# Splitting the first weight load and moving two small loads ahead of ScalarE's barrier

## The chip, the cores and the metric

The kernel runs on one core of a Trainium2 chip. The metric is the device time of one execution, in microseconds (us). The profile of an execution gives a span that is about 1.3 us shorter than its time (436.1 against 437.44 us for the first profiled execution). Repeated executions of one kernel agree within about 0.3%. A few lie near 445 us; they count as slow and are left out of every ratio. The medians quoted for a kernel are over all its runs; without the slow ones they would be lower by at most 0.27 us, which changes no verdict.

Short names: PE is TensorE's matmul side and PEld its weight loads, DVE is VectorE, ACT is ScalarE, POOL is GpSimd, SP is SyncE. A name with q (SPq, ACTq) is that engine's sequencer, which issues DMAs.

## The reference, cut to what matters

One decode step for 8 rows: a modulation computed from `c`, a grouped-query attention over a long cache, then a gated MLP.

```python
mod = (silu(c) @ w_mod)            # c: 8 x 1024, w_mod: 1024 x 6144, bf16: 12.6 MB
h = layernorm(x) * (1 + ca) + sa
q = h @ wq                         # 1024 x 4096: 8.4 MB
# attention: k and v caches of 8 x 4 x 8192 x 128 each: 134.2 MB together
x = x + ga * (attention(q, k_cache, v_cache) @ wo)      # wo: 8.4 MB
h = layernorm(x) * (1 + cb) + sb
x = x + gb * ((relu(h @ W_gate) * (h @ W_up)) @ W_down) # 3 x 7.3 MB
```

Every weight and cache byte is read once: 185.6 MB for 8 rows of output.

## The kernel before

All large loads go through one ring in SBUF (`arena`, 65,536 bf16 columns on 128 partitions). SyncE issues them in a fixed order: `w_mod` in two pieces of 6.29 MB, `wq` in two of 4.19 MB, then k and v by turns (16 pieces each of 4.19 MB), then `wo` and the MLP's weights. `pump` issues a load as soon as everything that lay in its part of the ring has been read.

```python
for i in range(2):
    load(("wm", i), wm_src[:, 24 * D * i:24 * D * (i + 1)], 24 * D)   # D = 1024
for i in range(2):
    load(("wq", i), wq_src[:, 2 * i * SLOT:2 * (i + 1) * SLOT], 2 * SLOT)
# ... k and v by turns, wo, gate, up, down ...
head = stream[1:]
del stream[1:]
pump()                                                    # first w_mod piece
for t, src in enumerate((c.rearrange(...), A_x.rearrange(...))):
    P.op("sp" if t == 0 else "act", lambda e, t=t, src=src: e.dma_start(cx[:, t, :], src), ...)
stream.extend(head)
P.pump = pump
pump()                                                    # second w_mod piece, first wq piece
```

The two `w_mod` pieces and the first `wq` piece fill the ring (24 + 24 + 16 thousand columns). The second `wq` piece needs the room of the first `w_mod` piece, so it waits until PE has done the first half of the modulation. The first k and v pieces wait for the second half. The modulation itself needs `c`: PE spreads c and x over the partitions with one matmul, DVE and ACT form silu(c) and its transpose and the first layer norm, and then come the modulation's 96 matmuls, 48 for each piece of `w_mod`.

`start_loads_first` moves SyncE's first DMA ahead of everything else on that engine and the next two ahead of its barrier instruction. So in the kernel before, SyncE's queue holds the first `w_mod` piece, then c, then the second piece. ScalarE issues x after the barrier.

Of the kernel before, what the change touches and what calls it, by code (L numbers as in the profile page):

```python
# [236 lines left out]
def start_loads_first(nc, n):  # L237

    block = nc.main_func.blocks[0]
    ins = list(block.instructions)  # L240
    sp = [i for i, x in enumerate(ins) if x.engine == mybir.EngineType.SP]
    at = next(i for i in sp if ins[i].opcode == "EventSemaphore")
    first = [ins[i] for i in sp if i > at][:n]
    assert all(x.opcode == "DMACopy" and not x.sync_info.on_wait for x in first), [x.opcode for x in first]
    names = {x.name for x in first}
    rest = [x for x in ins if x.name not in names]
    at = next(i for i, x in enumerate(rest) if x.engine == mybir.EngineType.SP and x.opcode == "EventSemaphore")
    rest = rest[:at] + first[1:] + rest[at:]
    at = next(i for i, x in enumerate(rest) if x.engine == mybir.EngineType.SP)
    block.instructions = rest[:at] + first[:1] + rest[at:]  # L250


def hold_weights(nc, held):
# [6 lines left out]
def bass_adaLN_cond__gqa_block_cached__glu_gated_reglu__decode_kernel(nc, A_x, A_k_cache, A_v_cache, A_wq, A_wo, B_x, B_W_gate, B_W_up, B_W_down, c, w_mod, out):  # L260
    B, _, D = A_x.shape
# [17 lines left out]
    P = Prog()  # L279
# [7 lines left out]
    with ExitStack() as es:  # L287
        E = es.enter_context

        def sb(name, shape, dtype):  # L290
            return E(nc.sbuf_tensor(name, shape, dtype))
# [15 lines left out]
        cx = sb("cx", [32, 2, 256], dt.bfloat16)  # L307
# [53 lines left out]
        def R(t, lo=0, hi=1):  # L361
            return (t, lo, hi)
# [9 lines left out]
        stream, place, cursor = [], {}, [0]  # L372

        def load(key, src, n):
            stream.append((key, src, n))

        def pump():
            while stream:
                key, src, n = stream[0]
                lo = cursor[0] if cursor[0] + n <= RING else 0  # L380
                if P.unread("arena", lo, lo + n):
                    return
                stream.pop(0)
                cursor[0] = lo + n
                place[key] = lo
                dst = arena[:, lo:lo + n]
                if len(src.shape) == 3:
                    dst = dst.rearrange("p (a n) -> p a n", a=src.shape[1])
                P.op("sp", lambda e, dst=dst, src=src: e.dma_start(dst, src), writes=[slot_r(lo, lo + n)], dma=True,
                     own=(key[0], key[1] % 2) if key[0] in "kv" else None)  # L390
                if key[0] in "kv":
                    P.held[key] = (lo, lo + n)

        wm_src = w_mod.rearrange("(p k) n -> p (k n)", k=KC)
# [2 lines left out]
        g_src = B_W_gate.rearrange("(p k) n -> p (k n)", k=KC)  # L397
        u_src = B_W_up.rearrange("(p k) n -> p (k n)", k=KC)
        d_src = B_W_down.rearrange("(p k) n -> p (k n)", k=KF)
        for i in range(2):  # L400
            load(("wm", i), wm_src[:, 24 * D * i:24 * D * (i + 1)], 24 * D)
        for i in range(2):
            load(("wq", i), wq_src[:, 2 * i * SLOT:2 * (i + 1) * SLOT], 2 * SLOT)
        for m in range(M):
# [9 lines left out]
        wd_parts = [(0, 14), (14, 21), (21, 25), (25, 27), (27, 28)]  # L414
        for i, (r0, r1) in enumerate(wd_parts):
            load(("wd", i), d_src[:, r0 * D:r1 * D], (r1 - r0) * D)
        head = stream[1:]
        del stream[1:]
        pump()
        for t, src in enumerate((c.rearrange("b (j n) -> (b j) n", j=4), A_x.rearrange("b o (j n) -> (b o j) n", j=4))):  # L420
            P.op("sp" if t == 0 else "act", lambda e, t=t, src=src: e.dma_start(cx[:, t, :], src), writes=[R("cx", t, t + 1)], dma=True)
        stream.extend(head)
        P.pump = pump
        pump()
# [120 lines left out]
        for z in range(2):  # L545
            src = ps[:, 3 + z, :].rearrange("p (u x r) -> p u r x", u=J, r=2)
# [14 lines left out]
        for u in range(4):  # L561
            src = ps[:, 5, :].rearrange("p (t j u b) -> p u b t j", t=2, j=J, u=4)[:, u]
# [152 lines left out]
        for z in range(2):  # L715
# [9 lines left out]
            else:  # L725
                P.op("act", lambda e, dst=dst, z=z: e.activation(dst, ps[:, z, :], ACT.Copy), reads=[bank(z)],
                     writes=[("kt", 512 * z, 512 * z + 512)])
# [22 lines left out]
        def row_turn(src, src_r, t):  # L750
# [6 lines left out]
             writes=[R("xg")])  # L757
# [15 lines left out]
        for h in range(2):  # L773
            P.op("act", lambda e, h=h: e.activation(grel[:, H * h:H * h + H], ps[:, h, 0:H], ACT.Relu), reads=[bank(h)],
                 writes=[("kt", 4096 + FJ * h, 4096 + FJ * h + FJ)])
# [26 lines left out]
        P.plan()  # L802
        P.emit(nc, dict(sp=nc.sync, act=nc.scalar, pool=nc.gpsimd, dve=nc.vector, pe=nc.tensor), sems)
        start_loads_first(nc, 3)
        hold_weights(nc, holding)

# [27 lines left out]
```

## Time and profile before

| | before |
|---|---|
| time, median of 3 runs | 437.1 us |
| span of the profiled execution | 436.1 us |
| bytes read | 185.63 MB |
| PE / DVE busy | 63% / 61% |
| SyncE's DMA queue, share of 16 engines | 98.8% |

These lines are from the page of the kernel before. The second line shown gives busy time, its share and the number of instructions for each engine. The GB/s line gives the DMA rate in 40 equal slices of the span (10.9 us each), and the last line gives SyncE's queue.

```profile
span 436.1 us, 3867 instructions
...
PE 275.4 (63%) x1643; PEld 119.1 (27%) x1483; DVE 265.6 (61%) x377; ACT 29.9 (7%) x62; POOL 14.5 (3%) x32
...
GB/s 407 425 418 433 431 433 433 434 433 431 433 433 433 433 433 433 433 433 433 433 433 433 433 433 433 433 433 433 436 433 433 433 433 433 450 429 422 428 429 211
...
q1 hardware_dynamic: 6848, 185.63, 98.8%
```

The rate stands at 433 GB/s in slice after slice, while neither PE nor DVE is busy two thirds of the time.

The chain of waits, followed back from the last instruction, reads quite differently (shares of the span by engine):

```profile
PE 42%; DVE 20%; issue 12%; DMA 6%; ACT 0%; SPq 0%
```

The start, from the timeline of the kernel before (start, duration, engine, line, operation, tiles; in brackets the idle time before it and what ended that):

```profile
0.00 0.38 SPq L389 DMA_DIRECT2D arena<-in_w_mod_dram  x1
...
0.63 0.34 SPq L421 DMA_DIRECT2D cx<-in_c_dram  x1
...
0.78 0.39 ACTq L421 DMA_DIRECT2D cx<-in_A_x_dram  x1
...
1.57 31.31 SPq L389 DMA_DIRECT2D arena<-in_A_wq_dram  x2
...
17.93 0.60 PE L450 MATMUL ps<-cx,rsel 32*128 32x512 bf16 x1 [17.93 <-DMA cx<-in_c_dram]
...
27.21 8.10 PE L516 MATMUL ps<-arena,hT 128*32 128x512 bf16 x96
...
32.31 0.11 PEld L516 LDWEIGHTS ps<-arena,hT 128*32 128x32 bf16 x4 [1.55 <-DMA arena<-in_w_mod_dram]
...
35.34 0.33 SPq L389 DMA_DIRECT2D arena<-in_A_k_cache_dram  x1
...
41.98 3.61 PE L539 MATMUL ps<-arena,hT 128*32 128x512 bf16 x32 [6.67 <-DMA arena<-in_A_wq_dram]
```

c is issued at 0.63 us but PE's first matmul (L450) waits for it until 17.93 us. The modulation (L516) starts at 27.21 us; its second half starts at 32.31 us. The first k load is issued at 35.34 us, and `wq`'s matmuls (L539) wait for their weights until 41.98 us. The `wq` line covers two issues, the first at 1.57 us and the second 31 us later.

From the issue lines of the DMA view (last number: us from issue to landing), and from the waits view (us in total, times, longest):

```profile
cx<-in_c_dram SPq DMA_DIRECT2D x1, 16.0 KB, 17.3
cx<-in_A_x_dram ACTq DMA_DIRECT2D x1, 16.0 KB, 9.6
```

```profile
PE ps L450 <- DMA cx<-in_c_dram: 17.9, 1, 17.9
...
DVE kt L581 <- DVEq L181: 16.7, 10, 2.7
```

The last waits line is DVE's wait for the landing of k (line 181 is the wait on a load's own semaphore): 16.7 us in all, in 10 of the 16 turns of the loop.

### The profile page before, as it was taken

How to read it: one execution, taken by the hardware profiler on the slowest of the kernel's cores; microseconds unless marked ns; L12 is line 12 of the kernel's file. 1: busy time of each engine (PE TensorE's matmuls, PEld its weight loads, DVE VectorE, ACT ScalarE, POOL GpSimd, SP SyncE). 2: the span in 40 equal slices, each digit the busy share in tenths (PEclk: the TensorE clock that was granted, in tenths of full speed). 3: DMA queues.
4: the chain of work that ended last, by engine and by line, in shares of the span. 5: the costliest groups of instructions: out<-in, count | busy, mean ns of one | idle time of the engine just before them, and what ended most of it. 6: DMA issues, size and time to landing. Idle time of an engine off the chain costs nothing.

```text
span 436.1 us, 3867 instructions
## 1 busy us (share of the span) xinstructions
PE 275.4 (63%) x1643; PEld 119.1 (27%) x1483; DVE 265.6 (61%) x377; ACT 29.9 (7%) x62; POOL 14.5 (3%) x32
## 2 busy tenths in 40 slices
PE   0063337759595957768595968768595958546437
PEld 0010002324242333324242333323242333242005
DVE  0233048687777867677787777678878676443020
ACT  1100010010101010010101010010101010110000
POOL 7000000000000000000000000000000000000000
PEclk9998569697978969696987969698887979867658
DMA  9999999999999999999999999999999999999995
GB/s 407 425 418 433 431 433 433 434 433 431 433 433 433 433 433 433 433 433 433 433 433 433 433 433 433 433 433 433 436 433 433 433 433 433 450 429 422 428 429 211
DMA packets 6934, 185.74 MB, mean 426 GB/s; under 512 B 816, under 2 KB 912, under 8 KB 1168
## 3 DMA queue, kind: packets, MB, share of 16 engines
q1 hardware_dynamic: 6848, 185.63, 98.8%
q8 instruction: 5, 0.08, 0.1%
q10 hardware_dynamic: 80, 0.02, 0.0%
q14 instruction: 1, 0.01, 0.0%
HBM read 185.63 MB, written 0.02 MB: 426 GB/s over the span
## 4 chain that ended last, share of the span: by engine, by line
PE 42%; DVE 20%; issue 12%; DMA 6%; ACT 0%; SPq 0%
PE ps L641 20%; PE ps L592 15%; DVE kt L581 9%; DMA arena<-in_B_W_down_dram 6%; DVE negm L604 5%; PE ps L610 2%; PE ps L658 1%; PE ps L769 1%; DVE om L652 1%; PE ps L738 1%; DVE mj L615 1%; DVE mjt L618 1%; DVE negm L608 1%; DVE kt L728 0%; DVE lx L701 0%
## 5 line engine op out<-in xcount | busy, mean ns | idle before, releaser
L581 DVE STREAM_TRANSPOSE kt<-arena 128x1024 uint32<-128x1024 uint32 x128 | 149.5, 1216 | 40.3 <-PE ps L592 23.3
L641 PE MATMUL ps<-arena,pT 128*64 128x512 bf16 x512 | 94.9, 551 | 52.1 <-issue 52.1
L592 PE MATMUL ps<-kt,qpad 128*128 128x512 bf16 x512 | 120.8, 382 | 10.0 <-DVE kt L581 8.6
L641 PEld LDWEIGHTS ps<-arena,pT 128*64 128x64 bf16 x512 | 45.3, 156 | 95.6 <-issue 90.9
L592 PEld LDWEIGHTS ps<-kt,qpad 128*128 128x128 bf16 x512 | 45.5, 97 | 83.9 <-DVE kt L581 29.1
L631 DVE STREAM_TRANSPOSE pT<-prb 64x1024 bf16<-64x1024 bf16 x32 | 39.7, 1239 | 18.1 <-ACT prb L624 17.6
L624 ACT ACTIVATE prb<-ps,bias 128x1024 bf16<-128x1024 f32 x16 | 17.8, 1113 | 293.0 <-DVE mjt L618 293.0
L604 DVE TENSOR_REDUCE negm<-ps 128x1 f32<-128x512 f32 x32 | 22.1, 690 | 11.6 <-PE ps L592 11.6
L652 DVE SCALAR_TENSOR_TENSOR om<-ps,im,om 128x128 f32<-128x128 f32 x51 | 17.7, 347 | 0.7
L769 PE MATMUL ps<-arena,hT 128*32 128x448 bf16 x128 | 11.7, 546 | 9.6 <-DMA arena<-in_B_W_up_dram 5.8
L610 PE MATMUL ps<-identf,negm 128*128 128x128 f32 x32 | 7.8, 326 | 15.6 <-DVE negm L608 15.6
L658 PE MATMUL ps<-jmp,om 128*128 128x16 f32 x34 | 6.7, 273 | 17.0 <-DVE om L652 17.0
L573 POOL TENSOR_TENSOR qpad<-qR,mq 128x128 bf16<-128x128 bf16 x16 | 6.3, 398 | 318.2 <-DVE pT L631 266.9
L539 PE MATMUL ps<-arena,hT 128*32 128x512 bf16 x64 | 7.2, 631 | 14.3 <-DMA arena<-in_A_wq_dram 14.3
L776 DVE TENSOR_TENSOR kt<-ps,kt 128x448 bf16<-128x448 f32 x2 | 1.2, 620 | 20.1 <-PE ps L769 20.1
L788 PE MATMUL ps<-arena,hmT 128*32 128x256 bf16 x112 | 8.8, 323 | 5.5 <-DMA arena<-in_B_W_down_dram 5.5
L452 DVE CAST cxr<-ps 128x512 bf16<-128x512 f32 x1 | 0.7, 691 | 18.6 <-PE ps L450 18.6
L450 PE MATMUL ps<-cx,rsel 32*128 32x512 bf16 x1 | 0.6, 604 | 17.9 <-DMA cx<-in_c_dram 17.9
L550 DVE CAST kt<-ps 128x512 bf16<-128x512 f32 x1 | 0.7, 692 | 17.9 <-PE ps L539 17.9
L610 PEld LDWEIGHTS ps<-identf,negm 128*128 128x128 f32 x32 | 4.7, 187 | 23.6 <-DVE negm L608 23.6
L658 PEld LDWEIGHTS ps<-jmp,om 128*128 128x128 f32 x34 | 5.1, 188 | 20.5 <-DVE om L652 20.5
L788 PEld LDWEIGHTS ps<-arena,hmT 128*32 128x32 bf16 x112 | 6.1, 114 | 9.0 <-DMA arena<-in_B_W_down_dram 7.4
(89 smaller groups left out, 96.3 us busy)
## 6 DMA issues: line engine op xcount, KB each, us to landing
arena<-in_A_k_cache_dram SPq DMA_DIRECT2D x16, 4096.0 KB, 21.5
arena<-in_A_v_cache_dram SPq DMA_DIRECT2D x16, 4096.0 KB, 19.6
arena<-in_w_mod_dram SPq DMA_DIRECT2D x2, 6144.0 KB, 24.5
arena<-in_A_wq_dram SPq DMA_DIRECT2D x2, 4096.0 KB, 30.5
arena<-in_A_wo_dram SPq DMA_DIRECT2D x2, 4096.0 KB, 18.1
arena<-in_B_W_gate_dram SPq DMA_DIRECT2D x2, 3584.0 KB, 16.5
arena<-in_B_W_up_dram SPq DMA_DIRECT2D x2, 3584.0 KB, 20.9
arena<-in_B_W_down_dram SPq DMA_DIRECT2D x1, 3584.0 KB, 21.8
```

The lines of the kernel that those rows point to most:

```text
L539: fns.append(lambda e, w=w, z=z, g=g, kk=kk: hold(e.matmul(ps[32 * g:32 * g + 32, 3 + z, :], hT[:, kk, :], w[:, g, z, :], start=(kk == 0), ...
L581: P.op("dve", lambda e: e.transpose(ktb[:, to:to + QE].bitcast(dt.uint32), arena[:, lo:lo + QE].bitcast(dt.uint32)), reads=[slot_r(lo, lo ...
L592: fns.append(lambda e, t=t, r=r: e.matmul(ps[:, b, :].rearrange("p (c k) -> p c k", k=32), qpad[:, m % 2, t * 2 + r, 24 - 8 * i:152 - 8 * ...
L604: P.op("dve", lambda e: e.tensor_reduce(negm[:, h:h + 1], ps[:, b, :], AX.X, ALU.max, negate=True), reads=[bank(b)] + (free(("v", m - 1)) ...
L610: P.op("pe", lambda e: e.matmul(ps[:, 4, 0:128], negm[:, 2:3].to_broadcast([128, 128]), identf[:], start=True, stop=True), reads=[R("negm" ...
L624: P.op("act", lambda e: e.activation(prb[:], ps[:, 2 * z:2 * z + 2, :].rearrange("p h n -> p (h n)"), ACT.Exp, bias=bias[:, z:z + 1], scal ...
L631: P.op("dve", lambda e, g=g: e.transpose(pT[64 * g:64 * g + 64, z, :, g, :], prb[64 * g:64 * g + 64, :]), reads=[R("prb")] + ([R("qpad", z ...
L641: fns.append(lambda e, t=t: e.matmul(ps[64 * (t % 2):64 * (t % 2) + 64, 5, :].rearrange("p (i d) -> p i d", d=Dh), pT[:, z, t].rearrange(" ...
L652: P.op("dve", lambda e, i=i: e.scalar_tensor_tensor(out=om[:], in0=ps[:, 5, Dh * i:Dh * i + Dh], scalar=im[:, i:i + 1], in1=om[:], op0=ALU ...
L658: P.op("pe", lambda e: e.matmul(ps[:, 6 + z, 0:16], om[:], jmp[:].rearrange("p g j -> p (g j)"), start=True, stop=True), reads=[R("om"), R ...
L769: fns.append(lambda e, w=w, r=kk - r0, kk=kk, h=h, j=j, b0=b0: hold(e.matmul(ps[32 * j:32 * j + 32, b0 + h, 0:H], hT[:, kk, :], w[:, r, j, ...
L788: fns.append(lambda e, w=w, r=k - r0, k=k, i2=i2, j=j: e.matmul(ps[32 * j:32 * j + 32, 4, 0:256], hmT[:, k, 1 - i2:33 - i2], w[:, r, i2, j ...
```

## The change

The intent is to let c and x land at once instead of behind 6 MB, so that the modulation can start earlier. The first piece of `w_mod` becomes two DMAs: 2 KB a row (256 KB in all) ahead of the remaining 46 KB a row. While the engines work on the short rows, c and x are to slip in from ScalarE's queue, on which they are now the very first instructions.

```diff
-    rest = rest[:at] + first[:1] ...            # SyncE only: 1 DMA ahead of all, n-1 ahead of the barrier
+    for engine, ahead, total in ((SP, 1, n), (Activation, 2, 2)):
+        ...                                     # the same for ScalarE: 2 DMAs ahead of all
...
-        for i in range(2):
-            load(("wm", i), wm_src[:, 24 * D * i:24 * D * (i + 1)], 24 * D)
+        load(("wm", 0), wm_src[:, 0:D], D)
+        load(("wm0", 0), wm_src[:, D:24 * D], 23 * D)
+        load(("wm", 1), wm_src[:, 24 * D:48 * D], 24 * D)
...
-        head = stream[1:]
-        del stream[1:]
+        head = stream[2:]
+        del stream[2:]
...
-            P.op("sp" if t == 0 else "act", lambda e, t=t, src=src: e.dma_start(cx[:, t, :], src), ...)
+            P.op("act", lambda e, t=t, src=src: e.dma_start(cx[:, t, :], src), ...)
```

(The hunks are shortened; the first says what the rewritten loop does.)

## The prediction

> **What bounds the kernel now.** The stream of loads. The page's DMA lines give 185.74 MB, 98.8% of 16 engines' span for SyncE's queue, and 433 GB/s in nearly every slice; PE is busy 63%, DVE 61%. The fabric ceiling of 435 GB/s (Trainium skill, "DMA: Bandwidth & Descriptors", Specifications) agrees with the 433 measured. 185.63 MB at 433 GB/s are 428.7 of the 436.1 us. The rest is at the ends: in the packet records the first weight packet starts 1.0 us after the first issue and takes 2.4 us where later ones of its size take 1.815 us; the last weight piece lands at 432.6 us and 3.5 us of work follow (chain of waits). In between no slice shows the queue empty: each load is issued some 20 us before it lands.
>
> **What the change does.** Today c is second in SyncE's queue, behind 6 MB, and lands at 17.9 us; x goes on ScalarE's queue after the barrier (issued at 0.78, landed about 10.1 us, since its 512 B packets alternate with 48 KB packets of 1.8 us). PE waits 17.9 us for c (waits view). Afterwards both are issued between 0.0 and 0.8 us on ScalarE's queue, while the other queue holds only the 256 KB piece, eight packets of 2 KB per engine (84 ns each in the last weight piece), because the rest is issued at about 0.63 us. Engines take queues in turn, packet by packet (same page, Queues, rings and completion order; the trace agrees), so c and x should land at 2.5 to 4 us, or up to 7 us if one or two 46 KB packets slip between.
>
> Costs: one more issue (0.38 us on SyncE); the small packets, an estimate of under 0.1 us (8 x 84 ns against 8 x 76 ns by bytes); the barrier is delayed by about 0.4 us by the two issues, which moves GpSimd's setup (rsel at 1.9 us, then 2.3) and the first wq issue. A gap of up to 0.3 us is possible if the small piece drains before the rest's descriptors are there.
>
> **How much is on the critical path.** Nearly nothing. PE's first matmul (cx by rsel) moves from 17.9 to about 3 us, and the transposed input of the modulation is ready near 8 us. The first half of the modulation matmuls then waits for its 6 MB; it starts near 17 instead of 27.2 us and ends near 21.5 instead of 32 us, and the second wq load is issued 10 us earlier. But the second half already waits 1.55 us for its weights, which land at 32.3 us because of 12.6 MB at 433 GB/s. So from 32 us on everything stands as before: modulation done at 35.3 us, first k load issued then, wq matmuls at 42 us on DMA. The earlier wq issue finds a queue not empty.
>
> **Prediction:** 437.0 us, 8 in 10 between 436.0 and 438.2. Faster by over 2%: 0.01; within 2%: 0.98; slower by over 2%: 0.01.
>
> **What would show each step.** Right: PE's cx matmul before 8 us; first modulation matmul at 16 to 19 us, waiting for weights instead of DVE; second half still at 32 to 33 us on a w_mod DMA; wq matmuls at about 42 us; 433 GB/s from the second slice on; last weight landing at 432 to 433 us. Wrong: cx still late; second half not on DMA; slice 0's rate changed by over 3%.
>
> **What would make it wrong.** A gap in the old stream that the slices hide and the earlier wq issue closes (gain up to 1 us); the small piece slowing the stream's start (loss up to 1 us); the span starting earlier because ScalarE's first issue precedes SyncE's.

## The result, and the profile after

The changed kernel took 436.83 us (median of 6 runs, 436.54 to 437.17), the kernel before 437.19 us over its 6 runs. The ratio of fast runs is 0.9995, with a 95% interval from 0.9982 to 1.0009. A ratio is the mean time of one kernel's fast runs over that of the other's fast runs in the same rounds, so it is not quite the ratio of the medians quoted. The verdict is: the same.

The page of the changed kernel:

```profile
span 435.6 us, 3869 instructions
...
PE 277.4 (64%) x1643; PEld 120.8 (28%) x1483; DVE 265.8 (61%) x377; ACT 29.9 (7%) x62; POOL 14.5 (3%) x32
...
GB/s 373 438 444 433 429 433 433 434 430 432 433 433 433 433 433 433 433 433 433 433 433 433 433 433 433 433 433 433 433 433 433 433 433 433 423 429 444 428 420 233
...
q1 hardware_dynamic: 6944, 185.61, 98.9%
```

Its start (line numbers are 5 higher than before, those of loads 4):

```profile
0.00 1.44 SPq L393 DMA_DIRECT2D arena<-in_w_mod_dram  x3
0.12 0.40 ACTq L426 DMA_DIRECT2D cx<-in_c_dram  x1
...
0.56 0.44 ACTq L426 DMA_DIRECT2D cx<-in_A_x_dram  x1
...
1.58 21.29 SPq L393 DMA_DIRECT2D arena<-in_A_wq_dram  x2
...
8.57 0.58 PE L455 MATMUL ps<-cx,rsel 32*128 32x512 bf16 x1 [8.57 <-DMA cx<-in_A_x_dram]
...
17.82 4.68 PE L521 MATMUL ps<-arena,hT 128*32 128x512 bf16 x48
...
31.74 4.54 PE L521 MATMUL ps<-arena,hT 128*32 128x512 bf16 x48 [9.24 <-DMA arena<-in_w_mod_dram]
...
36.33 0.33 SPq L393 DMA_DIRECT2D arena<-in_A_k_cache_dram  x1
...
41.40 3.60 PE L544 MATMUL ps<-arena,hT 128*32 128x512 bf16 x32 [5.11 <-DMA arena<-in_A_wq_dram]
```

The issue lines and waits that answer to those of before:

```profile
cx<-in_c_dram ACTq DMA_DIRECT2D x1, 16.0 KB, 2.9
cx<-in_A_x_dram ACTq DMA_DIRECT2D x1, 16.0 KB, 7.9
```

```profile
DVE kt L586 <- PE ps L597: 26.8, 14, 3.0
...
DVE kt L586 <- DVEq L181: 12.0, 9, 2.8
...
PE ps L521 <- DMA arena<-in_w_mod_dram: 9.2, 1, 9.2
...
PE ps L455 <- DMA cx<-in_A_x_dram: 8.6, 1, 8.6
```

c now lands about 3 us after the start and x at 8.5 us. PE's first matmul moves from 17.93 to 8.57 us, 9.4 us earlier, and the modulation's first half from 27.21 to 17.82 us. Then all of the gain turns into one new wait: PE stands 9.24 us before the second half, for the second piece of `w_mod`. That half starts at 31.74 us instead of 32.31, and the first k load is issued at 36.33 us, a microsecond *later* than before.

That last point is the clock. The granted clock (PEclk) is the share of TensorE's full clock that the chip let it have. The line below is from the table of stretches, for the stretch from 32.31 to 35.35 us; before:

```profile
core 0: us, PE busy (x) PEld busy (x) DVE busy (x) ACT busy (x) POOL busy (x), PEclk, DMA share, GB/s
32.31:35.35 3.04, 3.00 (x52) 0.42 (x16) 0.00 (x1) 0.00 (x1) 0.00 (x0) 1.00 0.80 345
```

and after:

```profile
32.31:35.35 3.04, 3.04 (x36) 0.49 (x12) 0.00 (x0) 0.00 (x0) 0.00 (x0) 0.50 0.87 377
```

The columns are those of the first line; the stretch itself and its length come first. The granted clock (PEclk, third number from the end) was 1.00 before and 0.50 after. (The view counts time before a trace's first clock record as 1.00. That record starts at 32.78 us in the kernel before and only at 47.42 us in c_at_32 below.) A matmul of the modulation took 634 ns at 0.50 and 379 ns at 1.00. Before, PE ran the two halves without a pause (the first 48 matmuls took 5.1 us, the last 48 about 3.0). After the change it stood idle for 9 us between them and started the second half slowly again: 4.54 us for 48 matmuls. The Trainium skill, "TensorE: Matmul & The Clock Gate" (Part 1), says that PE falls to half its clock after an idle window of about 3.4 us and needs about as long a busy one to return; the 9.24 us pause and the clock of 0.50 agree with it. In the clock records of the changed kernel the clock fell 2.6 us after the last matmul of the first half and came back 3.6 us after the second half began (3.6 and 5.2 us in its second trace). So the earlier work was not only useless here, it cooled PE. This costs nothing either, for `wq`'s matmuls still stand until 41.40 us for their own weights.

The span of this profiled execution is 0.5 us shorter than that of the first one of before, and several landings are about 0.5 us earlier. This is taken up in the last experiment.

### The profile page after: what moved, and what is told of

Read it like the earlier page. It is cut to its first block, busy times and chain, and to the rows that moved or that the text cites. A ratio compares the mean times of both kernels' runs of the same rounds, so it can differ in the third digit from the quotient of the medians.

```text
span 435.6 us, 3869 instructions
## 1 busy us (share of the span) xinstructions
PE 277.4 (64%) x1643; PEld 120.8 (28%) x1483; DVE 265.8 (61%) x377; ACT 29.9 (7%) x62; POOL 14.5 (3%) x32
## 3 DMA queue, kind: packets, MB, share of 16 engines
HBM read 185.63 MB, written 0.02 MB: 426 GB/s over the span
## 4 chain that ended last, share of the span: by engine, by line
PE 46%; DVE 20%; issue 13%; DMA 6%; ACT 0%; SPq 0%
PE ps L646 22%; PE ps L597 18%; DVE kt L586 9%; DMA arena<-in_B_W_down_dram 6%; DVE negm L609 5%; PE ps L615 2%; PE ps L663 2%; PE ps L743 1%; DVE om L657 1%; DVE mj L620 1%; PE ps L774 1%; DVE mjt L623 1%; DVE negm L613 1%; DVE kt L733 0%; DVE lx L706 0%
## 5 line engine op out<-in xcount | busy, mean ns | idle before, releaser
L586 DVE STREAM_TRANSPOSE kt<-arena 128x1024 uint32<-128x1024 uint32 x128 | 149.6, 1217 | 39.0 <-PE ps L597 26.8
L597 PE MATMUL ps<-kt,qpad 128*128 128x512 bf16 x512 | 122.4, 385 | 9.6 <-DVE kt L586 8.3
L774 PE MATMUL ps<-arena,hT 128*32 128x448 bf16 x128 | 9.4, 459 | 9.4 <-DMA arena<-in_B_W_up_dram 6.8
L544 PE MATMUL ps<-arena,hT 128*32 128x512 bf16 x64 | 7.1, 623 | 12.7 <-DMA arena<-in_A_wq_dram 12.7
L521 PE MATMUL ps<-arena,hT 128*32 128x512 bf16 x96 | 9.2, 565 | 9.2 <-DMA arena<-in_w_mod_dram 9.2
L528 DVE COPY mod<-ps 128x512 f32<-128x512 f32 x2 | 1.3, 671 | 17.8 <-PE ps L521 17.8
```

Of the source, the lines that this page charges most:

```text
L521: fns.append(lambda e, w=w, pr=pr, j=j, kk=kk: hold(e.matmul(ps[32 * j:32 * j + 32, pr, :], hT[:, kk, :], w[:, 2 * pr:2 * pr + 2, j, :], s ...
L586: P.op("dve", lambda e: e.transpose(ktb[:, to:to + QE].bitcast(dt.uint32), arena[:, lo:lo + QE].bitcast(dt.uint32)), reads=[slot_r(lo, lo ...
L597: fns.append(lambda e, t=t, r=r: e.matmul(ps[:, b, :].rearrange("p (c k) -> p c k", k=32), qpad[:, m % 2, t * 2 + r, 24 - 8 * i:152 - 8 * ...
L774: fns.append(lambda e, w=w, r=kk - r0, kk=kk, h=h, j=j, b0=b0: hold(e.matmul(ps[32 * j:32 * j + 32, b0 + h, 0:H], hT[:, kk, :], w[:, r, j, ...
```

## The experiments

Two theories stood against each other. *Stream*: the time is the bytes over 433 GB/s plus the two ends, and anything that leaves the DMA queue filled costs and gains nothing. *Chain*: PE and DVE set the pace, as the chain of waits has it, and the full queue is only a consequence of loads running ahead.

### Bytes in the middle of the loop (extra_mid)

One load that nothing waits for, added to the changed kernel in the middle of the attention loop:

```diff
+        junk = sb("junk", [128, 8 * D], dt.bfloat16)
...
                 stream.pop(0)
+                if key == ("k", 8):
+                    P.op("sp", lambda e: e.dma_start(junk[:], wm_src[:, 0:8 * D]), writes=[R("junk")], dma=True)
```

> The changed kernel with one load more: 2.10 MB into an unused buffer, issued in the middle of the attention loop, just before the ninth k load; nothing waits for it. Stream theory: bytes count one for one, 2.10 MB at 433 GB/s are 4.84 us: 441.3 to 442.0 us. Rival (PE and DVE set the pace of the loop, the loads run ahead by some 20 us and only look full): the queue absorbs it, 436.5 to 438 us.

It took 441.83 us (median of 4 runs), against 437.09 us for the changed kernel in the same call: 4.74 us more, where 2.10 MB at 433 GB/s are 4.84 us. Against the kernel before, the ratio is 1.0103 (1.0065 to 1.0141), clear of 1, though the rule with its 2% calls it unclear. The bytes count one for one, and the chain theory in its simple form falls. DVE's waits ahead of the transposes of k, 12.0 us for the landing and 26.8 us for PE in the changed kernel, become

```profile
DVE kt L589 <- DVEq L181: 29.2, 15, 5.2
...
DVE kt L589 <- PE ps L600: 13.1, 11, 2.3
```

Most of the longer wait for k only replaces a wait for PE: together they grow by 3.5 us. Where the time is decided is the end. In the packet records the last weight row ends at 437.20 us in place of 432.30 us, 4.9 us later, and in both kernels 3.3 us of work follow; so they do in the other six traces looked at (3.28 to 3.35 us).

Note how close the second limit is. In the changed kernel DVE waits only 12.0 us for k over 16 turns, some 0.75 us a turn of about 19.7 us (the mean distance of the turns in the chain of waits of before). That is why the chain of waits is full of PE and DVE: it follows the work that ended last at every step, and names the loads only where they were late. In the changed kernel's timeline the waits for k stop after 217 us: from there on the loop is behind its loads, and still the last weights decide the time.

### Two cuts that show when an early c is worth something (nowm1_before, nowm1_after, nowm1b_before, nowm1b_after)

If the second piece of `w_mod` is what swallows the gain, leaving it out should bring the gain to light. The cut gives a wrong result: the second half of the modulation reads the first half's weights. (The comparison with the reference still called the outputs correct; its tolerance is wider than what the modulation's second half changes.)

```diff
-        load(("wm", 1), wm_src[:, 24 * D:48 * D], 24 * D)
+        place["wm", 1] = 0
```

> Wrong result on purpose: the kernel before without the second w_mod load (6.29 MB less; the second half of the modulation reads the first half's weights). Theory: 6.29 MB at 433 GB/s are 14.5 us less by bytes, 422.6 us; but now the second half no longer waits for weights, so c's landing decides when the ring frees its room: the first k load is issued near 35 us, when the queue holds only 14.7 MB, drained at about 35.7 us. A small gap in the stream, 0.5 to 2 us: 423 to 424.7 us.

> Wrong result on purpose: the changed kernel without the second w_mod load. Theory: first k load issued near 26 us, no gap, so exactly the bytes are saved: 422.0 to 422.6 us, that is 0.5 to 2 us faster than the same cut of the kernel before, where the uncut pair differs by 0.3 us. Rival (the earlier c and x are worth nothing anywhere, or the time is not set by the stream's gaps): both cuts equal within 0.3 us, or a saving far from 14.5 us.

Both missed: 437.74 us for the cut of before (its six runs lay in two groups, near 435.7 and near 439.8 us, which was not looked into) and 436.21 us for the cut of the changed kernel, 14 us more than expected. One line of the latter's timeline shows that the edit was wrong, not yet the theory:

```profile
46.36 5.31 PE L521 MATMUL ps<-arena,hT 128*32 128x512 bf16 x48 [21.83 <-DMA arena<-in_A_k_cache_dram]
```

The second half waits for a load of *k*. The loads are issued while the program is being written down, after each PE operation; with the second half now reading the first piece's place, the first k load was put into that place before the second half was declared, and so the second half read k. The stream stood still meanwhile (1 GB/s between 46 and 57 us in both cuts). The mended cut holds the pump back for one step:

```diff
         for i in range(2):
+            P.pump = pump if i else None
             fns = []
```

> The cut of nowm1_before mended: there the first k load was put on the queue before the second half of the modulation was declared, so that half had to wait for k's landing (46.4 us) and the stream stood still from about 45 to 57 us. Now loads are pumped only after both halves. Wrong result on purpose. Stream theory: 6.29 MB less are 14.5 us less, 422.6 us, plus a small gap: the modulation ends near 35 us, its end frees the ring for the first k load, and what was issued before it (14.7 MB) is drained at about 35.7 us[...]: gap 0.3 to 1 us, so 422.9 to 423.6 us. Rival (the loop's chain of PE and DVE sets the pace, as the chain of waits would have it): also shorter, since the loop starts earlier; extra_mid tells these apart.

> The same mended cut of the changed kernel. Wrong result on purpose. Stream theory: the modulation ends near 26 us, the first k load is issued then, 9 us before the queue drains; no gap: 422.0 to 422.6 us, 0.5 to 1.3 us faster than the same cut of the kernel before. If the slack that the change adds is worth nothing here too: equal within 0.3 us.

| | uncut | cut | 6 runs of the cut |
|---|---|---|---|
| before | 437.35 | 423.35 | 422.71 to 424.32 |
| changed | 437.09 | 422.39 | 422.03 to 422.67 |

Both times fell where the stream theory had put them: the changed kernel lost 14.7 us (14.5 by bytes), and its cut is 1.0 us faster than the same cut of the kernel before. That is about what the change is worth once the weights no longer hide it. The timeline, cut of before and then of the changed kernel:

```profile
26.81 7.03 PE L517 MATMUL ps<-arena,hT 128*32 128x512 bf16 x96
...
33.87 0.33 SPq L389 DMA_DIRECT2D arena<-in_A_k_cache_dram  x1
```

```profile
18.00 7.30 PE L522 MATMUL ps<-arena,hT 128*32 128x512 bf16 x96
...
25.34 0.33 SPq L393 DMA_DIRECT2D arena<-in_A_k_cache_dram  x1
```

With c early, the modulation ends 8.5 us sooner and the first k load is issued at 25.34 instead of 33.87 us. Of these 8.5 us only about 1 us shows in the time, because the queue still had work until about 36 us. The stretch from 34 to 37 us, cut of before and then of the changed kernel (columns as above, the last is GB/s):

```profile
34.00:37.00 3.00, 0.31 (x8) 0.23 (x8) 2.86 (x6) 0.48 (x1) 0.00 (x0) 1.00 0.95 360
```

```profile
34.00:37.00 3.00, 0.00 (x0) 0.00 (x0) 0.00 (x0) 0.00 (x0) 0.00 (x0) 0.50 1.04 448
```

The rate falls to 360 GB/s in the first and stays full in the second (single stretches wobble, as whole packets are counted). By packet times 4.15 and 4.31 MB were moved between 30 and 40 us, which is a gap of about 0.4 us. This profiled execution of the cut of before was its fastest of six, with the same span as the other cut; the difference of 1.0 us rests on the six runs of each, which do not overlap, and not on this one trace. The uncut pair differs by 0.3 us, which its runs do not resolve.

### How late may c be? (c_at_22, c_at_32)

The kernel before with c put behind a third of the second `w_mod` piece, and behind all of it:

```diff
 # c_at_22
-        for i in range(2):
-            load(("wm", i), ...)
+        load(("wm", 0), wm_src[:, 0:24 * D], 24 * D)
+        load(("wm", 1), wm_src[:, 24 * D:32 * D], 8 * D)
+        load(("wm1", 1), wm_src[:, 32 * D:48 * D], 16 * D)
 # both
-        head = stream[1:]
-        del stream[1:]
+        head = stream[2:]
+        del stream[2:]
```

> The kernel before with c later: the second w_mod piece is split 8:16 and c is issued between, so that it lands near 22 us instead of 17.9. Theory (the stream bounds, and c has slack): from the trace, the second wq load is issued 14.6 us after c lands (17.93 to 32.55) and has to be on the queue [...]before the stream runs out of what was issued before it, at about 40.5 us; so c may land until about 24.4 us at no cost. Here: same time, 436.5 to 437.6 us, though the modulation ends about 4 us later. Rival (the start of the kernel is a chain in which c's landing counts one for one, hidden by something else in the changed kernel): slower by about 4 us.

> The kernel before with c behind both w_mod pieces: lands near 32.3 us, 14.4 us later than before. Theory: beyond the slack of about 6.5 us the DMA queue runs empty before the second wq load is issued (near 47 us, the queue drained at about 40.5), so the stream loses about 7 to 8 us: 444 to 446 us, with a gap in the DMA rate between 40 and 48 us. Rivals: chain, one for one, 451 us; no dependence at all, 437 us.

c_at_22 took 437.22 us (ratio 1.0006, 0.9991 to 1.0020): no change, although PE's first matmul came at 22.51 us and the first k load was issued at 39.03 us:

```profile
22.51 0.60 PE L451 MATMUL ps<-cx,rsel 32*128 32x512 bf16 x1 [22.51 <-DMA cx<-in_c_dram]
...
39.03 0.33 SPq L389 DMA_DIRECT2D arena<-in_A_k_cache_dram  x1
```

c_at_32 took 444.42 us (ratio 1.0173, 1.0158 to 1.0188), 7.5 us more for a c that came 14.3 us later than in the kernel before:

```profile
1.57 45.57 SPq L389 DMA_DIRECT2D arena<-in_A_wq_dram  x2
...
32.20 0.60 PE L450 MATMUL ps<-cx,rsel 32*128 32x512 bf16 x1 [32.20 <-DMA cx<-in_c_dram]
...
41.47 8.28 PE L516 MATMUL ps<-arena,hT 128*32 128x512 bf16 x96
```

The second `wq` load could be issued only at 46.8 us, and its first packet started at 47.8 us; meanwhile the queue had run dry (stretches of the same execution, columns as in the table of stretches above, last column GB/s):

```profile
41.00:47.00 6.00, 6.00 (x57) 1.22 (x22) 0.32 (x2) 0.20 (x1) 0.00 (x0) 1.00 0.00 0
47.00:50.00 3.00, 2.75 (x48) 0.32 (x12) 0.21 (x1) 0.21 (x1) 0.00 (x0) 1.00 1.00 339
```

Over the 8 us from 40 to 48 us the mean rate is 53 GB/s, so the stream lost 8 x (1 - 53 / 433) = 7.0 us there.

So c was already inside its slack before the change. Up to somewhere past 22 us it costs nothing, and beyond that it costs about the time that the queue stands empty. (The 24.4 us and the slack of 6.5 us in the two expectations are estimates that allow 1.5 us for a new load to start; c_at_32 shows 1.0 us, which would make them 24.9 and 7.0 us.) The change lengthened a slack that was not used.

### The parts of the change (split_only, order_only, first_8k)

```diff
 # split_only: kernel before, with only (4 DMAs moved ahead in place of 3, so that both w_mod pieces stay there)
+        load(("wm", 0), wm_src[:, 0:D], D)
+        load(("wm0", 0), wm_src[:, D:24 * D], 23 * D)
 # order_only: changed kernel, with the first piece whole (and the counts of loads moved ahead to fit)
+            load(("wm", i), wm_src[:, 24 * D * i:24 * D * (i + 1)], 24 * D)
 # first_8k: changed kernel, with
+        load(("wm", 0), wm_src[:, 0:4 * D], 4 * D)
+        load(("wm0", 0), wm_src[:, 4 * D:24 * D], 20 * D)
```

> The split alone, c and x issued as before (c behind the first 6 MB on SyncE's queue, x on ScalarE's after the barrier). Theory (bound by the stream): same time, 436.5 to 437.3 us; c lands near 17.5 us and PE's cx matmul stands there. If the small piece is what evens the engines' start (theory A of before_again), the last engine closes the first 12.6 MB at most 0.4 us behind the one before it, and the kernel is 0.3 to 0.5 us faster than before.

> c and x first on ScalarE's queue ahead of its barrier instruction, the first 6 MB whole. Theory: each engine serves the queues in turn, so each of the 6 packets of c and x (two rows and one semaphore write each) waits for a 48 KB packet of 1.8 us: x lands at 1.0 + about 6 x 1.8 = 12 us (11 to 14), PE's cx matmul there, and the time is the same, 436.5 to 437.3 us. Rival (the split is not needed to get c and x in early): x lands before 6 us.

> The changed kernel with a first piece of 8 KB a row instead of 2 KB. In the changed kernel x missed the small packets (its first row at 4.03 us, behind a 46 KB packet) and landed at 8.5 us. Theory: with eight packets of 309 ns an engine the small piece lasts until about 3.7 us, x alternates with those, lands by 4.5 us, PE's cx matmul stands before 5 us, and the modulation's first half then waits for its 6 MB and not for DVE, starting near 16.6 us instead of 17.8; the time stays within 0.1% of the changed kernel, because the second half still waits for its weights until about 31.7 us. Rival (x is late for another reason, such as a late issue): x still lands at 8 us or later.

| | time, median | ratio to before, 95% | PE's first matmul |
|---|---|---|---|
| before | 437.18 | | 17.93 us |
| split_only | 436.96 | 0.9999 (0.9985 to 1.0013) | 17.38 us |
| order_only | 437.38 | 1.0005 (0.9991 to 1.0019) | 14.09 us |
| first_8k | 436.69 | 0.9994 (0.9981 to 1.0008) | 9.69 us |

All are the same in time, as expected. For PE's first matmul both parts are needed to come to 8.57 us. order_only, with 48 KB rows of 1.8 us each in the way:

```profile
14.09 0.58 PE L454 MATMUL ps<-cx,rsel 32*128 32x512 bf16 x1 [14.09 <-DMA cx<-in_A_x_dram]
```

The packet records show c's two rows and its semaphore write, then x's, each taking one turn against a 48 KB row: x ends at 13.6 us. The Trainium skill, "DMA: Bandwidth & Descriptors" (Queues, rings and completion order), says that an engine serves its queues in turn, a packet at a time; the runs agree, with the packet here a whole row of 48 KB.

first_8k missed. With 8 KB rows (309 ns each) lasting until about 4.2 us, x was expected by 4.5 us. It landed at 9.3 us, and PE stood until 9.69 us:

```profile
9.69 0.58 PE L455 MATMUL ps<-cx,rsel 32*128 32x512 bf16 x1 [9.69 <-DMA cx<-in_A_x_dram]
```

In the packet records of both the changed kernel and first_8k, c's rows slip in among the short rows, and x's first row starts one long packet after c's semaphore write (at 4.0 to 4.7 us and at 5.6 to 6.2 us). Why x never catches the short rows, issued only 0.44 us after c, was not settled. In first_8k the short rows lasted to the end of c's turn and some 0.6 us past it (c's semaphore writes at 3.5 to 4.1 us, the last short rows until 4.1 to 4.7 us), so their length alone does not explain it. In the kernel before, x was alone on its queue and issued at 0.78 us, and yet its first row came only at 5.1 us, after two long rows; so x's packets may become ready late, which no run here separates.

### Is the half microsecond real? (before_again, after_again)

The two first traces differed by 0.5 us in span. In the packet records of the kernel before, one DMA engine began its first packet 0.46 us after the first one and took 3.15 us for it, and the landings after it closed late: the last engine ended the first 12.6 MB 0.9 us after the one before it, and `wq`'s first piece likewise.

> The kernel before, unchanged, for a second trace. Both theories: the same time within 0.1%. What it tells: in the first trace of this kernel one DMA engine began its first packet 0.46 us after the others and took 3.15 us for it (the others about 2.4), so it closed the first 12.6 MB at 31.91 us where the next one closed at 30.98; in the changed kernel's trace the last engine closed at 31.37 and the one before at 31.16. Theory A (a late engine at the start is a property of a start on 48 KB rows): again one engine about 0.9 us behind, second half of the modulation at 32.3 us. Theory B (chance of one execution): the lag differs, anywhere between 0.2 and 1 us.

> The changed kernel again, for a second trace and five rounds more. First piece whole (three traces): the last DMA engine closed the first 12.6 MB at 31.91, 31.40 and 31.73 us; small first piece (three traces): 31.37, 31.37, 31.35. If the small piece evens the start: again 31.3 to 31.5 us. If chance: anything between 31.3 and 31.9. Either way the time is within 0.15% of before, 436.5 to 437.2 us.

The end of the first 12.6 MB on the last engine, from the packet records:

```
first piece whole : before 31.91, before_again 31.40, order_only 31.73 us
first piece small : split_only 31.37, changed 31.37, first_8k 31.35, after_again 31.56, extra_mid 31.53 us
```

before_again has a span of 435.6 us, the same as the changed kernel's first trace: the half microsecond was an execution with a late engine. The two rows of numbers overlap. The small piece may even out the start a little, by one or two tenths (c_at_22, with a whole first piece, has 31.69 us, c included); neither these traces nor the times (0.9995, 0.9966 to 1.0023 in the second comparison) settle it. The times were 436.98 us for before_again and 437.09 us for after_again. They were run at other times.

## Why the prediction was right

The time was predicted at 437.0 us and measured at 436.83 us, and "within 2%" was right. Point by point:

- **The stream of loads bounds the kernel: shown.** 2.10 MB more cost 4.74 us (4.84 by bytes), 6.29 MB less saved 14.7 us (14.5 by bytes). Where the queue ran dry for about 7 us the time grew by 7.5 us.
- **The second half of the modulation waits for its weights, so an earlier c gains nothing: shown.** PE waits 9.24 us there now. Without those weights the change is worth about 1 us. (The 1.55 us that the prediction read as this wait in the kernel before were idle time of the weight-load side; PE itself did not wait yet.)
- **The earlier second `wq` load finds a queue that is not empty: shown.** It is issued 10.0 us earlier (at 22.5 instead of 32.5 us), and the rate of the stream does not change.
- **c at 2.5 to 4 us: right (3.0). x at up to 7 us: wrong (8.5 us).** Consequently PE's first matmul came at 8.57 us, not before 8, and the modulation's first half, at 17.82 us, still waited for the layer norm on DVE and not for its weights. That it fell in the range foreseen (16 to 19 us) is in part luck: PE was through with the layer norm's matmuls 0.9 us after the weights had landed (16.9 us). The step that failed is that x, too, would slip in while the short rows last; first_8k shows that longer short rows do not mend it. It cost nothing, since the second half's weights came later still.
- **Modulation done at 35.3 us, first k load issued then: wrong by 1.0 us (36.33).** The prediction took the second half's 3.0 us from a warm PE; after the 9 us pause it took 4.54 us at a clock of 0.50.
- **The second half at 32 to 33 us, `wq` at 42 us, last weights at 432 to 433 us:** 31.74, 41.40 and 432.30 us, the first two about half a microsecond earlier than written; the unchanged kernel's second trace has 41.47 us for `wq` too.
- **A rate in slice 0 changed by over 3% as a sign of error: a badly chosen sign.** The page shows 407 and then 373, but before_again shows 390 for the unchanged kernel. By packet times, 3.55 MB were moved in the first 10 us before and 3.52 MB after.

No version tried that loads all the weights beats both kernels beyond the noise. What is left beside the stream is 1.0 us until the first packet and 3.3 us after the last weight row.

## What to carry to other kernels

Before moving work earlier, find the next thing that the moved work will wait for; if that is a landing in a stream that never pauses, the gain ends there, and an idle PE may start the next stage at half its clock. A small load's landing matters only when it delays the issue of the next large load past the moment at which the queue runs dry; compute that slack from the trace first. To decide between a full DMA queue and a chain of waits that names the engines, add a load that nobody waits for and see whether its bytes come back in the time.

## What the Trainium skill lacked or had wrong

- "DMA: Bandwidth & Descriptors" (Bandwidth, Where 436 GB/s comes from) says that for loads from HBM a limit of about 358 GB/s per core binds. Here one core read 185.63 MB from HBM at 433 GB/s in the steady slices, 426 GB/s over the span, close to the fabric ceiling of about 435 GB/s that the same page gives. The sentence needs the condition that both cores of a pair stream, which the page's table of measurements and "HBM Reference" do state: a core that streams alone gets well above its share.
- The same page (Specifications) gives about 0.6 us to the first byte for DMAs from the SyncE and ScalarE queues, and does not say from when it counts. In these traces the first packet starts 0.62 us after the end of the issuing instruction where the queue was empty (SyncE's first DMA, 0.38 to 1.00 us; the second `wq` load of c_at_32, 47.14 to 47.76 us), which is 1.0 us after its start. c's first packet on ScalarE's queue came 1.36 us after its issue ended (0.52 to 1.88 us), with other packets under way.
- No page says what a small DMA on a second queue pays for landing beside long rows. Here each of its rows and its semaphore write took a turn against one long packet: with 48 KB rows of 1.8 us, c and x on one queue landed at 13.6 us, and x took 7.9 us from issue to landing even in the changed kernel.
- No page gives how much one DMA engine that starts late can delay the landings behind it: 31.91 us in place of 31.40 us for the first 12.6 MB in two traces of the same kernel.
